# Staging buffers for the first MLP's weights, and the rank of attention's loads, in a fused attention and two-MLP kernel

## The chip, the cores and the metric

The kernel runs on one core of a Trainium2 chip. The metric is the device time of one execution in microseconds. In the profile PE is TensorE (matmuls; PEld are its weight loads), DVE is VectorE, ACT is ScalarE, POOL is GpSimd, and SP is SyncE, which here issues nearly all DMAs.

## What is computed

The reference, cut to what matters (the token axis is B * S = 2304, the model axis H * D = 512):

```python
def attn(q, k, v, M_prev, z_prev, beta):          # B, H, S, D = 4, 8, 576, 64
    scores = where(causal, -1e9, q @ k.T / sqrt(D))
    a = softmax(scores)                            # over the keys
    local = a @ v
    q_p = phi(q)                                   # x > 0 ? x + 1 : exp(x)
    mem_out = (q_p @ M_prev) / (q_p @ z_prev + 1e-6)
    g = sigmoid(beta)
    return g * mem_out + (1 - g) * local

x = attn(...).transpose(0, 2, 1, 3).reshape(2304, 512)
h = x @ w_in;   x = (h * sigmoid(h)) @ w_out              # 512 -> 2048 -> 512
h = x @ w_in2;  y = (h * tanh(softplus(h))) @ w_out2
```

## The kernel before

**An order written out beforehand.** The program adds its operations to a plan, each with a priority (the smallest goes first), the engines that could do it with a cost, and the data that it writes and reads. `Plan.issue` then plays the plan through once with these costs and fixes the order of instructions on every engine. On an engine, that which is ready earliest goes first, and of several that are ready the one with the lowest priority value. A DMA is issued on SP as soon as its data and its destination are free, by the same rule; in the plan, transfers follow each other at 360 bytes per ns. The order is fixed when the program is built; on the chip each engine takes its instructions in that order and waits where an input is late.

**Attention** goes in visits of a pair of heads: 16 visits to the first 256 queries (two steps of 128 each), then 16 to the rest (three steps). For a visit, `load_kq` loads keys and queries and `load_vm` values and memory matrix, each into one of a few buffers; the loads for visit v + 1 are asked for in the first step of visit v. A step has three stages: scores, their softmax and a DMA transposition of the result (`stage_a`), the second product three steps later (`stage_b`), the output (`stage_c`). Results go through the DRAM tensor `xd`. Attention's priorities are `att_prio(n) = 2.3 * n`, some -1.5e5 lower for the first eight steps, which are those that chunk 0 of the MLP needs.

**The MLPs** take the 2304 tokens in nine chunks of 256 each. For a chunk, `chunk_x` loads x from `xd` and splits it in a high and a low half (f16); eight times per chunk `gemm1` makes two blocks of hidden units, `hidden` their activation, and `gemm2` adds their product into the output. Their matmuls have the priorities 1e6 and up, so they fill TensorE where attention leaves it free; all the rest of an MLP has -1e6 and up, ahead of attention.

**The weights** of each MLP come as 16 units of 1 MB in a 64-bit format, eight for the first matrix (k = 0) and eight for the second (k = 1). `weight_unit` loads a unit into a staging buffer of 8 KB per partition and turns it into f32 in six passes on ScalarE and VectorE, the last of which takes the largest square sum and writes into the staging buffer; its result stands in `slot(l, u + 2)` of the MLP's weight tile. When the eight units of a half are there, `weight_scale` finds a scale for all of them, and `weight_split` writes unit u as two f16 halves into `slot(l, u)`, reading `slot(l, u + 2)`. So the weight tile `w` has 18 slots, and those of the late units lie empty at first. The units of the first MLP have priorities -2e5 + u (first half, ahead of attention) and -1e5 + u (second half, behind the first eight steps of attention and ahead of the later ones); those of the second MLP 1e5 + u, into a tile that takes attention's place.

The staging buffers are two rings: the first half of the first MLP takes the two buffers `ws` and two places in the tiles `g` and `xh`, which are not used yet; everything else takes turns in the two of `ws`. The change touches the rings (line 237), the choice of a ring in `weight_unit` (line 660) and the priorities of the two loads in `attention` (lines 787 and 792).

Of the kernel before, what the change touches and what calls it, by code (L numbers as in the profile page):

```python
# [9 lines left out]
F32 = mybir.dt.float32  # L10
F32R = mybir.dt.float32r
U32 = mybir.dt.uint32
# [26 lines left out]
NU = NF  # L39
SPARE = 2  # L40
# [138 lines left out]
def attn_moe_moe2_kernel(ctx: ExitStack, tc: tile.TileContext, kq, vm, beta, w1, w2, out):  # L179
# [22 lines left out]
    def buf(name, shape, dt, n=1):  # L202
        ts = [sb.tile([128, *shape], dt, name=f"{name}_{i}") for i in range(n)]
        return ts

    def ring(tiles):
        state = [0]

        def take():
            state[0] += 1  # L210
            return tiles[(state[0] - 1) % len(tiles)]

        return take
# [14 lines left out]
    w_first, = buf("w", [(NU + SPARE) * 2048], F16)  # L228
# [5 lines left out]

    ws = buf("ws", [1024, 2], U32, 2)
    early = [t[:, 0:4096].bitcast(U32).rearrange("p (n t) -> p n t", t=2) for t in (g_tile, xh)]
    wstages = [ring(ws + early), ring(ws)]
    ga = buf("ga", [2 * TOK], F32, 2)

    spares = [w_first[:, 2048 * NU + 1024 * i:2048 * NU + 1024 * i + 1024].bitcast(F32) for i in range(2 * SPARE)]  # L240
# [55 lines left out]
    def slot(l, u):  # L296
        return (w_first, w_second)[l][:, 2048 * u:2048 * u + 2048]
# [38 lines left out]
    def act(prio, out, in_, func, scale=1.0, bias=0.0):  # L336
        plan.add(prio, [c_act(out, in_, func, scale, bias)], [out], aps(in_, scale, bias) + [tables])

    def ts(prio, out, in0, s1, op0, s2=None, op1=None):
        plan.add(prio, [c_ts(out, in0, s1, op0, s2, op1)], [out], aps(in0, s1), shared=not ps(in0))  # L340

    def stt(prio, out, in0, s, in1, op0, op1):
        plan.add(prio, [c_stt(out, in0, s, in1, op0, op1)], [out], aps(in0, s, in1), shared=not ps(in0) and not ps(in1))

    def tt(prio, out, in0, in1, op, es=("DVE",)):
        plan.add(prio, [(*c_tt(e, out, in0, in1, op), WAIT_R * i) for i, e in enumerate(es)], [out], aps(in0, in1),
                 shared=not ps(in0) and not ps(in1))
# [34 lines left out]
    def dma(prio, out, in_, writes=None, reads=None):  # L382
        nbytes = 128 * cols(out) * SIZE[out.dtype]
        plan.add(
            prio, [("SP", 475, lambda: nc.sync.dma_start(out=out, in_=in_))],
            [out] if writes is None else writes, [in_] if reads is None else reads, tail=nbytes / 360)
# [49 lines left out]
    def load_kq(v, prio):  # L436
        p, _, nk = VISITS[v]
        n = min(S, 128 * nk)
        t = kqr()
        rk[v], rq[v] = t[:, 0, 0:n], t[:, 1]  # L440
        dma(prio, t[:, :, 0:n], kq[p].rearrange("p (t s) -> p t s", t=2)[:, :, 0:n], reads=[])

    def load_vm(v, prio):
        p, _, nk = VISITS[v]
        n = nk * 2 * (D + 1)
        t, rm[v] = rvr()[:, 0:n], rmr()
        rv[v] = t.rearrange("p (n e d) -> p n e d", n=nk, e=2)
        dma(prio, t, vm[p, :, 130:130 + n], reads=[])
        dma(prio, rm[v], vm[p, :, 0:130], reads=[])
# [43 lines left out]
    def prep_phi(v, i0, i1, prio):  # L493

        if v not in er:
            er[v] = er_()
        e, src = er[v][:, 64 * i0:64 * i1], rq[v][:, 64 * i0:64 * i1]
        act(prio, e, src, AF.Exp)
        act(prio, src, src, AF.Relu)
        stt(prio, e, e, 1.0, src, ALU.min, ALU.add)  # L500
# [65 lines left out]
    def stage_b(n, prio):  # L566

        v, qt = STEPS[n]
        R = min(128, S - 128 * qt)
        nk = qt + 1  # L570
        v1, v2, gvv = vv[v]
        vb = bank[6 + qt % 2]
        if qt < 4:
            pw = pts.pop(n).rearrange("p (s e k) q -> p s k e q", s=2, e=2)
        else:
            pw = pts.pop(n).rearrange("p (s k) (e q) -> p s k e q", s=2, e=2)
        ms = []
        for e in range(2):
            o = vb[0:R, 65 * e:65 * e + 65]
            for kb in range(nk):  # L580
                hi, lo = pw[:, 0, kb, e, :], pw[:, 1, kb, e, :]
                ms += [
                    (o, hi, v1[:, kb, e, :], kb == 0, False),
                    (o[:, 0:D], hi, v2[:, kb, e, :], False, False),
                    (o, lo, v1[:, kb, e, :], False, kb == nk - 1)]
        mm(prio, ms + [(vb[0:R, 130:260], er[v][:, 128 * qt:128 * qt + R], rm[v], True, True)])
        if not last(n):
            return
        m = 1 + qt % 2
        g = banks[0:R, 512 * 6:512 * 8].rearrange("p (b c) -> p b c", b=2)[:, 0:m, 0:260].rearrange("p b (a c) -> p b a c", a=4)  # L590
        den, t4, x = denr()[0:R, 0:m], t4r()[0:R, 0:m], xr()[0:R, 0:m]
        each = lambda y: y[0:R].unsqueeze(1).to_broadcast([R, m, 4])
        tt(prio, den, g[:, :, :, D], each(eps), ALU.add)
        other(prio, "DVE", 165, lambda: nc.vector.reciprocal(out=den, in_=den), [den], [den])
        tt(prio, den, den, each(gvv), ALU.mult)
        tt(prio, t4, g[:, :, :, 0:D], den.unsqueeze(3).to_broadcast([R, m, 4, D]), ALU.mult)
        tt(prio, x, t4[:, :, 0:2], t4[:, :, 2:4], ALU.add, ("POOL", "DVE"))
        xts[n] = (x, R)

    def stage_c(n, prio):  # L600

        if not last(n):
            return
        v, qt = STEPS[n]
        p = VISITS[v][0]
        x, R = xts.pop(n)
        m = 1 + qt % 2
        for i in range(m):
            x2, o = x[:, i].rearrange("p e d -> p (e d)"), bank[6 + i][:, 260:260 + R]
            plan.add(prio, [("PE", 56, lambda o=o, x2=x2: nc.tensor.transpose(o, x2, ident[0:R, 0:R]))], [o], [x2, ident],  # L610
                     edge=(107, 56))
        xo = xor_()[:, 0:m * R]
        copy(prio, xo.rearrange("p (b c) -> p b c", b=m),
             banks[:, 512 * 6:512 * 8].rearrange("p (b c) -> p b c", b=2)[:, 0:m, 260:260 + R])
        b, hp = divmod(p, H // 2)
        t0, n = column(b, 256 * (qt // 2)), m * R
        dma(prio, xd[128 * hp:128 * hp + 128, t0:t0 + n], xo, writes=[("xd", hp, hp + 1, t0, t0 + n)])
# [35 lines left out]
    def weight_unit(l, u, prio):  # L653

        r, w = wstages[int(l > 0 or u >= NU // 2)](), slot(l, u + SPARE).bitcast(F32)  # L660
        t = w.bitcast(U32)
        dma(prio, r, W[l][u].bitcast(U32).rearrange("p (n t) -> p n t", t=2), reads=[])
        low, high = r[:, :, 0], r[:, :, 1]
        act(prio, w, high.bitcast(F32), AF.Abs, 2.0**-112)
        ts(prio, t, t, 3, ALU.logical_shift_left)
        stt(prio, t, high, 0x80000000, t, ALU.bitwise_and, ALU.bitwise_or)
        act(prio, low, low, AF.Copy, 2.0**-29)
        tt(prio, t, t, low, ALU.add, ("DVE", "POOL"))
        top = topw[l][:, u:u + 1]

        plan.add(prio, [("ACT", 0.833 * 1024 + 200, lambda: nc.scalar.activation(  # L671
            out=low.bitcast(F32), in_=w, func=AF.Square, accum_out=top))], [top, low], [w, tables])
# [91 lines left out]
    A_RATE, MOE_B, L_V = 2.3, -1e6, 0.0  # L764
    att_prio = lambda n, d=0: A_RATE * (n + d) + (ATT_B if n < N0 else 0)
# [9 lines left out]
    def attention(n0, n1, sbs):  # L775

        for n in range(n0, n1):
            if 0 <= n - LAG - 1 < NS:
                stage_c(n - LAG - 1, att_prio(n - LAG - 1, D_C))
            if 0 <= n - LAG < NS:  # L780
                stage_b(n - LAG, att_prio(n - LAG, D_B))
            if n < NS:
                pr_ = att_prio(n)
                v, qt = STEPS[n]
                qts = VISITS[v][1]
                if qt == qts[0] and v + 1 < len(VISITS):
                    load_kq(v + 1, pr_)
                stage_a(n, sbs, pr_)
                if qt == qts[0]:
                    prep_v(v, att_prio(n, D_B) - D_V)  # L790
                    if v + 1 < len(VISITS):
                        load_vm(v + 1, att_prio(n, L_V))
                if qt == 0 and 2 in qts:
                    prep_q(v, 1, att_prio(n + 2) - D_Q)
                if qt == qts[0]:
                    prep_phi(v, 2 * qts[0], min(2 * qts[-1] + 2, S // 64), att_prio(n, D_B) - D_P)
                if qt == qts[-1] and v + 1 < len(VISITS):
                    prep(v + 1, att_prio(n + 1) - D_K)
# [20 lines left out]
    while n_att < N0:  # L819
        attention(n_att, n_att + 1, s_all)  # L820
        n_att += 1
# [96 lines left out]
```

## Time and profile before

| | us |
|---|---|
| time, median of 3 runs (1025.13 to 1026.48) | 1025.33 |
| the profiled execution: time | 1025.4 |
| the profiled execution: span from the first to the last instruction | 1023.6 |
| PE busy | 948.2 (93%) |
| PEld busy | 732.2 (72%) |
| DVE busy | 673.4 (66%) |
| ACT busy | 642.5 (63%) |
| POOL busy | 273.9 (27%) |

The mean granted clock of TensorE is 0.960 of full speed. Busy shares are means over stages that differ; where the time goes is read from the slices of the span, the table of windows and the waits.

### The profile page before, as it was taken

Reading aid. Unit: us, or ns where it says so; the run is one execution under the profiler, and the core shown is the slowest. Engines: PE = TensorE matmul, PEld = TensorE weight load, DVE = VectorE, ACT = ScalarE, POOL = GpSimd, SP = SyncE. Lnnn points to the kernel's source line nnn. Section 1 sums busy time; section 2 is a strip of 40 time slices with the busy share of each in tenths; the row PEclk is TensorE's granted clock in tenths of the full one; section 3 lists DMA queues with packets and bytes.
Section 4 is the critical chain, followed back from the end, with each engine's and each line's share of the span. In section 5 each row is a group of like instructions: output and inputs, shape, how many; then the busy total and the mean of one; then the engine's idle time right before and its main releaser. Section 6 shows DMA issues by size and latency. Waiting matters only on the chain.

```text
span 1023.6 us, 20794 instructions
## 1 busy us (share of the span) xinstructions
PE 948.2 (93%) x8364; PEld 732.2 (72%) x8364; DVE 673.4 (66%) x1231; ACT 642.5 (63%) x1095; POOL 273.9 (27%) x280
## 2 busy tenths in 40 slices
PE   2436589999999999999999999999999999999998
PEld 1225478888888888888888888766676766766665
DVE  6988687787787878777757756754544545544433
ACT  7977665666666756756667676744555545555544
POOL 1110123343343433432322522212212122222221
PEclk9956589999999999999999999999999999999999
DMA  9767924775787767845353341100100101000000
GB/s 322 230 148 208 228 58 114 162 187 133 183 156 150 151 137 148 176 114 130 105 199 104 104 146 61 42 30 14 42 22 21 32 12 42 22 21 22 1 21 21
DMA packets 149904, 107.93 MB, mean 105 GB/s; under 512 B 111152, under 2 KB 139312, under 8 KB 145712
## 3 DMA queue, kind: packets, MB, share of 16 engines
q1 hardware_dynamic: 149664, 106.60, 40.1%
q8 instruction: 65, 1.06, 0.4%
q14 instruction: 31, 0.25, 0.1%
q10 hardware_dynamic: 144, 0.00, 0.0%
HBM read 66.21 MB, written 14.16 MB: 79 GB/s over the span
## 4 chain that ended last, share of the span: by engine, by line
PE 85%; DMA 6%; DVE 4%; ACT 4%; issue 1%; SPq 0%; POOL 0%; DVEq 0%; POOLq 0%; ACTq 0%
PE banks L375 84%; DMA arena<-arena 2%; DVE w L322 1%; PE banks L610 1%; DMA g<-w 1%; ACT w L314 1%; DMA xs<-xd 1%; ACT arena L314 1%; DMA ws<-w 1%; DVE arena L322 1%; DMA arena<-kq 1%; ACT ws L671 0%; DVE w L328 0%; DVE arena L328 0%; DMA arena<-vm 0%
## 5 line engine op out<-in xcount | busy, mean ns | idle before, releaser
L375 PEld LDWEIGHTS <-w 128*128 128x128 f16 x3456 | 334.8, 98 | 43.3 <-issue 4.2
L375 PEld LDWEIGHTS <-arena 128*128 128x128 f16 (+1 forms) x3168 | 225.5, 101 | 80.1 <-DMA arena<-arena 27.5
L328 POOL TENSOR_TENSOR g<-ga,g 128x512 f16<-128x512 f32 x108 | 144.1, 1335 | 345.7 <-ACT g L314 327.4
L375 PE MATMUL banks<-xh,w 128*128 128x256 f16 x1728 | 213.8, 275 | 2.6 <-DVE ga L322 2.6
L375 PE MATMUL banks<-g,w 128*128 128x256 f16 x1728 | 209.8, 273 | 0.1
L375 PE MATMUL banks<-xh,arena 128*128 128x256 f16 x1728 | 198.6, 273 | 0.0
L375 PE MATMUL banks<-arena,g 128*128 128x512 f16 x864 | 197.4, 379 | 0.0
L375 PE MATMUL banks<-arena 128*128 128x65 f16 (+6 forms) x1728 | 119.0, 235 | 62.1 <-DMA arena<-arena 24.1
L375 PEld LDWEIGHTS <-g 128*128 128x128 f16 x864 | 84.5, 98 | 87.6
L314 ACT ACTIVATE ga<-ga 128x512 f32<-128x512 f32 x108 | 67.6, 628 | 77.5 <-DVE ga L319 53.6
L314 ACT ACTIVATE arena<-arena 128x256 f32<-128x256 f32 (+6 forms) x180 | 101.5, 592 | 18.5 <-PE banks L375 9.5
L322 DVE SCALAR_TENSOR_TENSOR ga<-ga,banks 128x512 f32<-128x512 f32 x108 | 73.7, 683 | 54.2 <-ACT ga L314 53.7
L322 DVE SCALAR_TENSOR_TENSOR arena<-arena 128x256 f16<-128x256 f32 (+6 forms) x144 | 106.1, 746 | 3.9 <-ACT arena L314 3.4
L314 ACT ACTIVATE w<-w 128x512 f32<-128x512 f32 x108 | 66.6, 625 | 47.3 <-DVE w L319 26.3
L314 ACT ACTIVATE arena<-banks,arena 128x128 f32<-128x128 f32 (+4 forms) x144 | 73.9, 545 | 33.9 <-DVE arena L546 25.9
L314 ACT ACTIVATE g<-ga 128x512 f16<-128x512 f32 x106 | 66.3, 626 | 28.7 <-DVE ga L322 28.2
L328 POOL TENSOR_TENSOR arena<-arena 128x256 f32<-128x256 f32 (+1 forms) x48 | 44.0, 916 | 139.1 <-DVE arena L328 89.3
L314 ACT ACTIVATE ga<-banks,xsc 128x512 f32<-128x512 f32 x72 | 49.2, 685 | 49.2 <-PE banks L375 45.5
L546 DVE TENSOR_REDUCE arena<-banks 128x2 f32<-128x256 f32 (+3 forms) x80 | 64.3, 804 | 23.8 <-PE banks L375 19.9
L328 POOL TENSOR_TENSOR g<-w,g 128x512 f16<-128x512 f32 x36 | 41.6, 1156 | 126.2 <-ACT g L314 126.2
L375 PEld LDWEIGHTS banks<-arena 128*128 128x128 f32 (+2 forms) x288 | 42.4, 228 | 32.9 <-ACT arena L314 29.6
L319 DVE TENSOR_SCALAR ga<-banks,xsc 128x512 f32<-128x512 f32 x36 | 27.0, 750 | 51.7 <-PE banks L375 51.6
(95 smaller groups left out, 942.0 us busy)
## 6 DMA issues: line engine op xcount, KB each, us to landing
ws<-w SPq DMA_DIRECT2D x28, 1024.0 KB, 5.3
arena<-kq SPq DMA_DIRECT2D x16, 576.0 KB, 5.0
arena<-vm SPq DMA_DIRECT2D x16, 325.0 KB, 3.4
xs<-xd SPq DMA_DIRECT2D x9, 512.0 KB, 4.6
yd<-w SPq DMA_DIRECT2D x36, 128.0 KB, 1.9
xs<-yd SPq DMA_DIRECT2D x9, 512.0 KB, 3.8
arena<-kq SPq DMA_DIRECT2D x16, 256.0 KB, 3.4
xd<-arena SPq DMA_DIRECT2D x32, 128.0 KB, 2.5
```

Of the source, the lines that this page charges most:

```text
L314: return ("ACT", ns, lambda: nc.scalar.activation(out=out, in_=in_, func=func, scale=scale, bias=bias))
L319: return ("DVE", ns, lambda: nc.vector.tensor_scalar(out=out, in0=in0, scalar1=s1, scalar2=s2, op0=op0, **kw))
L322: return ("DVE", 1.04 * cols(out) + 160, lambda: nc.vector.scalar_tensor_tensor(out=out, in0=in0, scalar=s, in1=in1, op0=op0, op1=op1))
L328: return (e, ns, lambda: eng.tensor_tensor(out=out, in0=in0, in1=in1, op=op))
L375: nc.tensor.matmul(out=o, lhsT=l, rhs=r, start=a, stop=z)
L546: other(prio, "DVE", 1.04 * cols(both) + 146, lambda: nc.vector.tensor_reduce(out=m1, in_=both, axis=AX, op=ALU.max, negate=True), [m1], [ ...
L610: plan.add(prio, [("PE", 56, lambda o=o, x2=x2: nc.tensor.transpose(o, x2, ident[0:R, 0:R]))], [o], [x2, ident], edge=(107, 56))
```

## The change

The ring of the first MLP's staging buffers becomes a written list of 16 places, one for each unit in turn. `room[0]` to `room[4]` are pairs of slots of the weight tile itself: slots 8 and 9, 10 and 11, 12 and 13, 14 and 15, 16 and 17. Units 0 to 7 go to the two of `ws`, to `g` and `xh`, and to `room[1]` to `room[4]`, so each has a place of its own. Units 8 to 15 go to `ws` (2), `room[3]`, `room[4]`, `room[0]`, `ws` (2) and `room[0]`. A place in `room` can be loaded when what stood in its slots has been read: `room[0]` after the splits of units 6 and 7 and, the second time, after unit 12. The second MLP's units take turns in the two of `ws`, as before. And the two loads of attention for the next visit get priorities that are lower by 1e6, which puts them ahead of the weights' loads wherever both are ready.

```diff
     ws = buf("ws", [1024, 2], U32, 2)
     early = [t[:, 0:4096].bitcast(U32).rearrange("p (n t) -> p n t", t=2) for t in (g_tile, xh)]
-    wstages = [ring(ws + early), ring(ws)]
+
+    room = [w_first[:, 2048 * i:2048 * i + 4096].bitcast(U32).rearrange("p (n t) -> p n t", t=2) for i in range(8, NU + SPARE, 2)]
+    wstages = [ring(ws + early + room[1:] + ws + [room[3], room[4], room[0]] + ws + [room[0]]), ring(ws)]
...
-        r, w = wstages[int(l > 0 or u >= NU // 2)](), slot(l, u + SPARE).bitcast(F32)
+        r, w = wstages[l](), slot(l, u + SPARE).bitcast(F32)
...
                 if qt == qts[0] and v + 1 < len(VISITS):
-                    load_kq(v + 1, pr_)
+                    load_kq(v + 1, pr_ - 1e6)
                 stage_a(n, sbs, pr_)
                 if qt == qts[0]:
                     prep_v(v, att_prio(n, D_B) - D_V)
                     if v + 1 < len(VISITS):
-                        load_vm(v + 1, att_prio(n, L_V))
+                        load_vm(v + 1, att_prio(n, L_V) - 1e6)
```

## Rows read from the trace of the kernel before

**Rows 1.** Page, the span in 40 slices, busy tenths of TensorE.

```profile
PE   2436589999999999999999999999999999999998
```

**Rows 2.** Windows: us, then busy time and instructions of each engine.

```profile
9.00:60.00 51.00, 19.07 (x117) 12.63 (x118) 47.86 (x86) 50.10 (x82) 2.92 (x5) 0.88 0.78 252
60.00:118.00 58.00, 33.82 (x216) 23.60 (x215) 47.85 (x102) 41.08 (x78) 7.02 (x10) 0.56 0.75 207
118.00:131.60 13.60, 6.51 (x40) 4.33 (x41) 7.61 (x30) 7.48 (x14) 1.29 (x3) 0.50 0.86 189
131.60:200.00 68.40, 68.08 (x660) 56.75 (x659) 51.85 (x117) 42.17 (x90) 19.64 (x21) 0.97 0.49 113
```

The columns of such a row are PE, PEld, DVE, ACT and POOL, then the granted clock, the DMA share and GB/s.

**Rows 3.** Waits of TensorE from 131 us on: total, times, longest.

```profile
PE banks L375 <- DVE ga L322: 2.6, 1, 2.6
```

**Rows 4.** Chain that ended last: start, length, what, four of its pieces.

```profile
3.54 10.51 DMA g<-w
...
102.48 7.48 DMA ws<-w
...
114.34 6.75 DMA arena<-arena
...
131.59 26.32 PE banks L375 x229
```

**Rows 5.** Timeline of TensorE: start, length, instruction; GEMM1 of chunk 0.

```profile
93.38 5.74 PE L375 MATMUL banks<-xh,w 128*128 128x256 f16 x42
```

**Rows 6.** Timeline of SP: weight loads and the first transposition.

```profile
2.59 0.91 SPq L385 DMA_DIRECT2D ws<-w  x2
...
4.01 0.43 SPq L385 DMA_DIRECT2D xh<-w  x1
...
14.11 3.75 SPq L559 DMA_TRANSPOSE arena<-arena  x2
...
36.04 0.33 SPq L385 DMA_DIRECT2D ws<-w  x1
...
66.01 0.35 SPq L385 DMA_DIRECT2D ws<-w  x1
...
102.48 0.34 SPq L385 DMA_DIRECT2D ws<-w  x1
```

**Rows 7.** Staging tile, 60 to 118 us: ns min/median/max, first and last start.

```profile
L671 ACT ACTIVATE ws<-w x8: 1108/1146/1167, 64.8 to 116.6; 128x1024 f32<-128x1024 f32 x8
L671 ACT ACTIVATION_READ_ACCUMULATOR ws<-w x8: 178/192/212, 65.8 to 117.6; 128x1 f32 x8
```

**Rows 8.** Waits of ScalarE, 60 to 118 us.

```profile
ACT ws L671 <- DVE w L328: 4.8, 3, 3.1
ACT w L314 <- DMA ws<-w: 4.6, 4, 2.7
```

**Rows 9.** Waits of VectorE, 60 to 118 us.

```profile
DVE w L328 <- ACT ws L314: 2.5, 2, 1.5
...
DVE w L319 <- ACT w L314: 1.2, 2, 1.1
```

**Rows 10.** Windows of attention's tile alone, columns as in rows 2.

```profile
60.00:118.00 58.00, 24.70 (x148) 16.50 (x141) 23.15 (x71) 17.80 (x47) 7.02 (x10) 0.56 0.75 207
...
131.60:200.00 68.40, 17.93 (x184) 11.82 (x178) 29.74 (x83) 22.77 (x59) 5.71 (x11) 0.97 0.49 113
```

**Rows 11.** Windows of the mask's tile alone: TensorE, then POOL.

```profile
60.00:118.00 58.00, 3.44 (x18) 0.00 (x0) 0.56 0.75 207
...
131.60:200.00 68.40, 3.14 (x22) 0.00 (x0) 0.97 0.49 113
```

**Rows 12.** Tile of x (a staging place), 0 to 20 us: its load.

```profile
DMA to landing us min/median/max: 12.5/12.5/12.5
```

**Rows 13.** Timeline of ScalarE: the first pass over a unit.

```profile
9.15 1.12 ACT L314 ACTIVATE w<-ws 128x1024 f32<-128x1024 f32 x1 [1.79 <-DMA ws<-w]
```

**Rows 14.** Tile of the scales: of the second MLP, on VectorE.

```profile
L641 DVE RECIPROCAL wsc<-cvec x2: 144/148/153, 549.4 to 629.3; 128x1 f32<-128x1 f32 x2
```

**Rows 15.** Attention's tile, 636 to 700 us: GEMM2 of the second MLP.

```profile
L375 PE MATMUL banks<-arena,g x116: 378/379/380, 653.5 to 699.9; 128*128 128x512 f16 x116
```

**Rows 16.** Timeline of TensorE: the first product with transposed data.

```profile
19.70 1.10 PE L375 MATMUL banks<-arena 128*128 128x65 f16 x8 [12.54 <-DMA arena<-arena]
```

**Rows 17.** Timeline of VectorE: the first use of that product's result.

```profile
37.81 0.16 DVE L328 TENSOR_TENSOR arena<-banks,eps 128x8 f32<-128x8 f32 x1
```

## The prediction

> **What bounds the kernel now.** I read the page's slices first, to see where TensorE is not full; then a table of windows, the waits, and the chain that ended last. TensorE is nearly idle or half busy in the first five or so slices of the span and full in almost all the rest [rows 1]. In numbers: it is busy 33.82 of 58 us between 60 and 118 us, 6.51 of 13.6 us up to 131.6 us, and 68.08 of 68.4 us after that [rows 2]. After 131 us its longest wait is 2.6 us [rows 3]. So once the first MLP runs, the remaining work of TensorE sets the end, and only two things can move it: the moment at which the MLP becomes able to fill TensorE (131.6 us now), and how much attention has been done by then.
>
> What sets that moment is the preparation of the first MLP's weights. The chain of waits runs through the load of a late unit (7.48 us at 102.48), then through a transposition for the last attention step that delays the scale of the second half (6.75 us at 114.34), to the unbroken run of matmuls at 131.59 [rows 4]. The first hidden activations were ready to be computed long before: GEMM1 of chunk 0 starts at 93.38 [rows 5]. GEMM2 lacks the second half of the weights.
>
> **What the loads cost now.** The first four loads are issued from 2.59 us on; the second half has two buffers, so after the load at 36.04 the next can be issued only at 66.01, and the last of the half at 102.48 (six loads in 36.5 us) [rows 6]. All eight units of that half have their square sums between 65.8 and 117.6 us [rows 7]. In 60 to 118 us ScalarE waits 4.6 us for such loads and 4.8 us for VectorE's step of the same unit, and VectorE 2.5 and 1.2 us for ScalarE's steps of the same unit [rows 8, 9]: with one unit at hand at a time, the two engines wait for each other. VectorE, the fuller one, is busy 47.85 of 58 us there, so 10.15 us are idle [rows 2].
>
> **The change, part by part.**
>
> *Five buffers in the second half.* Units 8 and 9 go to the two old buffers, 10 and 11 to places that hold staged units 6 and 7 before, so all four can be in place before 60 us. Unit 12 needs the splits of units 6 and 7, units 13 and 14 need 8 and 9 done, unit 15 needs unit 12. From 60 us on there are two or more units to choose from until the last. The gain is bounded below by nothing, if attention's own chain is what VectorE really follows, and above by the whole idle time, 10.15 us. The two waits on ScalarE for the same unit make 3.7 us of it; the rest are waits in attention, which a second unit at hand can fill. I take the middle, 7 us, and leave 3 us for unit 15, whose load and steps come one after the other.
>
> *Attention moved behind the weights.* The second half is ranked ahead of attention from step 8 on. Now it can use that rank, so some steps move past the start of the MLP. In 60 to 118 us VectorE spends 23.15 us on attention [rows 10] for nine steps (18 mask matmuls, two to a step) [rows 11]: 2.6 us each. In 131.6 to 200 us TensorE spends 17.93 us [rows 10] on eleven steps (22 mask matmuls) [rows 11]: 1.63 us each, at the full clock. Every step moved frees 2.6 us before the start and costs 1.63 us after it: 0.95 us gained. If no step moves, the term is 0; if eight do (8 to 15, which no one needs until chunk 1), 7.6 us. I take four: 3.9 us.
>
> *Eight buffers in the first half.* All eight loads are issued at once. Two neighbours at the start land 2.46 us apart (3.54 + 10.51 = 14.05 us for the third [rows 4]; 4.01 + 12.5 = 16.5 us for the fourth [rows 6, 12]). ScalarE has three passes over a unit, the last of them 1.15 us long [rows 7], and is 50.10 of 51 us busy between 9 and 60 us [rows 2]; the loads do not hold it up, so earlier ones give nothing there: 0. If its cover, the full ScalarE, were gone, a gain of at most the 0.9 us of idle time in that window would be had.
>
> *Attention's loads first.* At the start the load of visit 1's keys and queries, its values and its memory matrix, and one memory matrix more go ahead of the first weight: four more issues of some 0.47 us (two weights take 0.91 us in [rows 6]), 1.9 us. The first weight's pass starts at 9.15 us after a wait of 1.79 us for the load [rows 13], so it becomes some 1.8 us later. Visit 1's own passes are then there to fill ScalarE, so the cost lies between 0 and 1.8 us; I take 1.8. Later in the kernel the rank only decides which of several ready loads goes first on SP; after 131 us TensorE never idles over 2.6 us at once [rows 3], so I put nothing there, at most that wait.
>
> The sum is made against the profiled execution, 1025.4 us (span 1023.6), within 0.1 us of the median of 1025.33: 1025.4 - 7.0 - 3.9 + 1.8 = 1016.3 us.
>
> **What is late next.** The second MLP's weights. The scale of their second half is ready at 629.3 us [rows 14], its first GEMM2 starts at 653.5 us [rows 15]. The scale, then a split, leaves about 20 us. A start of the MLP 9 us earlier uses half of this.
>
> **A row and a rule that speak against it.** The first transposition is issued at 14.11 us, when four loads of 1 MB are under way [rows 6], and TensorE waits 12.54 us for it, until 19.70 [rows 16]; the fourth load landed at 16.5. So a transposition waits for what is queued in front of it. With eight loads in front, at 2.46 us each, the queue ends about four loads or 9.8 us later, and the first transpositions and visit 2's load land near 30 us. VectorE needs the first result of attention's second product only at 37.81 us now [rows 17], so 8 us of cover remain, and the sum puts nothing on it.
>
> The Trainium skill, page "DMA: Bandwidth & Descriptors", section "Queues, rings and completion order", says that each DMA engine consumes a queue's descriptors in ring order. By that rule, ranking attention's loads first helps only those that are ready before the weights are issued; the trace agrees as far as the 12.54 us go. The sum by it would be that of the rival of the queue, below.
>
> **Rivals.**
>
> *The queue (slower).* The order on each engine is written out beforehand. If an attention instruction that depends on a late transposition stands ahead of weight passes on VectorE or ScalarE, these wait behind it. It decides from a stall of 9.1 + 2.05 = 11.2 us on. That would need the 9.8 us of additional queue to hit an engine with no cover, and once more for visit 2 or 3, say 13 us together: 1025.4 - 9.1 + 13 = 1029 us. For it: 12.54 us of such a wait exist already. Against: it falls on TensorE, which has nothing else to do, and the 8 us of cover. 0.14.
>
> *Attention bounds the start (same).* Steps 0 to 7 slide by the queue's 9.8 us, and with them x of chunk 0 (GEMM1 at 93.38 becomes 103) and everything ranked below; the units fill holes but the start stays within 2 us of 131.6, at 1025 us. Against: attention is ranked ahead of the second half and finds free engines earlier, as the first half's units end sooner. 0.12.
>
> *Second MLP late (smaller gain).* Attention ends later by more than the 20 less 9 us of slack; each microsecond above is lost. With 5 lost, 1021 us. Against: attention keeps its rank, and VectorE has a quarter of its time free in 131.6 to 200 us (51.85 of 68.4 us busy, [rows 2]). 0.12.
>
> *All of it (larger gain).* All 10.15 us close, eight steps move, and the early loads cost nothing: 1025.4 - 10.15 - 7.6 = 1007.6 us. 0.17.
>
> The forecast's own case has 0.45, between 1011 and 1020 us.
>
> **How the numbers follow.** The likeliest is 1016.3 us. The range has to hold 8 in 10: with 0.10 left out at the top (most of the queue's case) and little below, it runs from 1007 to 1027 us. A measurement of this kernel tells 0.2% from no change, here 2.05 us. Faster than 1023.3 us: the forecast's 0.45, the larger gain's 0.17, the late second MLP's 0.12, 0.74 in all. Slower than 1027.4: 0.14. Same: 0.12.
>
> **What the profile after would show.** Right: loads of the second half issued before 60 us, the last of the eight done near 100 us rather than 118, the unbroken run of matmuls from about 115 us, full TensorE from there to the end, and fewer mask matmuls before that start. ScalarE's waits for loads and for VectorE's step of the same unit near nothing. Wrong: the run starting after 125 us; idle VectorE or ScalarE behind a transposition between 15 and 45 us; a wait of TensorE for a split of the second MLP near 640 us; or the start moved by as much as forecast with as many microseconds of deferred attention on TensorE behind it.

## The result, and the profile after

The changed kernel takes 1016.73 us (median of 4 runs, 1014.98 to 1017.62), beside 1025.88 us for the kernel before: ratio 0.9909, 95% interval 0.9891 to 0.9927. The forecast was 1016.3 us. The profiled execution took 1014.98 us, span 1013.1 us, 10.5 us less than the span of before. Line numbers after the added lines are 2 higher, so helper L375 is now L377.

The windows of the kernel after (columns as in [rows 2]):

```profile
9.00:60.00 51.00, 13.93 (x89) 9.51 (x89) 45.85 (x81) 47.80 (x74) 3.32 (x5) 0.92 0.92 285
60.00:97.00 37.00, 12.24 (x81) 8.33 (x82) 35.18 (x62) 29.85 (x49) 4.53 (x5) 0.50 0.74 230
60.00:118.00 58.00, 32.16 (x260) 24.16 (x261) 52.16 (x101) 46.66 (x79) 10.78 (x10) 0.66 0.61 180
112.60:200.00 87.40, 84.27 (x817) 69.71 (x816) 59.81 (x153) 55.48 (x128) 23.02 (x29) 0.96 0.53 118
```

From 60 us until the last unit is done (97 us), VectorE is busy 35.18 of 37 us; before it left 10.15 of 58 us idle up to 118 us [rows 2]. But TensorE, full from the MLP's start on before, now has 3.13 us of holes between 112.6 and 200 us, and a mean granted clock of 0.96 there.

Where the units went: the square sums of the second half (staging places in `ws`, then those in the weight tile), first and last start in 60 to 100 us, on ScalarE:

```profile
L673 ACT ACTIVATION_READ_ACCUMULATOR ws<-w x4: 180/186/216, 69.2 to 91.9; 128x1 f32 x4
...
L673 ACT ACTIVATION_READ_ACCUMULATOR w<-w x4: 176/182/190, 76.3 to 96.5; 128x1 f32 x4
```

The last one starts at 96.5 us, 21 us earlier than the 117.6 of [rows 7]. The waits of ScalarE that answer to [rows 8], in 60 to 109 us:

```profile
ACT w L316 <- DMA w<-w: 2.2, 1, 2.2
...
ACT w L673 <- DVE w L330: 1.4, 2, 0.8
```

Once for a load (2.2 us, unit 15) instead of 4.6 us, and 1.4 us instead of 4.8 for VectorE's step of the same unit. The waits of VectorE for ScalarE's steps of the same unit, 2.5 and 1.2 us in [rows 9], are one of 0.2 us in the same window:

```profile
DVE w L321 <- ACT w L316: 0.2, 1, 0.2
```

GEMM2 of chunk 0, the first matmul from `g`, in 90 to 145 us, in the kernel before and after:

```profile
L375 PE MATMUL banks<-g,w x54: 272/273/273, 138.5 to 144.9; 128*128 128x256 f16 x54
```

```profile
L377 PE MATMUL banks<-g,w x131: 269/273/273, 112.6 to 144.9; 128*128 128x256 f16 x131
```

It starts 25.9 us earlier, and the span shrinks by 10.5. The other 15.4 us are found with two more views. First, the mask's matmuls up to GEMM2's start, two to a step of attention (columns as in [rows 11]), before and after:

```profile
0.00:138.50 138.50, 7.68 (x40) 0.97 (x4) 0.70 0.73 214
```

```profile
0.00:112.60 112.60, 5.21 (x28) 0.97 (x4) 0.79 0.78 238
```

14 steps have been begun instead of 20. Six steps at the prediction's 1.63 us are, by estimate, 9.8 us of TensorE's time that now lie behind the start. Second, the windows of 152 to 168 us, after:

```profile
152.00:156.00 4.00, 3.27 (x34) 2.57 (x32) 1.43 (x4) 2.32 (x5) 0.17 (x1) 1.00 1.55 210
156.00:160.00 4.00, 1.96 (x8) 1.17 (x8) 3.43 (x7) 1.86 (x6) 0.37 (x1) 0.74 0.57 136
160.00:164.00 4.00, 3.78 (x28) 2.78 (x29) 2.53 (x14) 3.52 (x7) 0.79 (x1) 0.50 0.25 66
164.00:168.00 4.00, 4.00 (x35) 3.43 (x34) 2.96 (x7) 2.21 (x7) 0.93 (x2) 0.91 0.57 135
```

and TensorE's timeline there:

```profile
156.26 0.95 PE L377 MATMUL banks<-arena 64*128 64x256 f32 x4 [0.99 <-ACT arena L316]
157.14 0.28 PE L377 MATMUL banks<-mask,ident 128*128 128x128 bf16 x2
159.04 0.79 PE L377 MATMUL banks<-diag,onesf 128*128 128x128 f32 x2 [1.61 <-DVE diag L330]
```

The matmul with `diag` belongs to the scale of chunk 1's x (`largest`). That x had its load issued only at 151.06 us, since the steps it needs came late. 3.0 us are idle in these four windows: 1.61 us before the matmul with `diag`, and 0.99 us before a step of attention that waits for ScalarE. (That chunk 1's matmuls would have filled the second hole, had x been there, is argued and not shown by itself.) The granted clock falls to 0.50 (the 1.2 GHz level) between 160 and 164 us. By estimate, at the clock of these windows the busy time loses 1.96 x 0.26 + 3.78 x 0.50 + 4.00 x 0.09 = 2.8 us. So 25.9 - 9.8 - 3.0 - 2.8 = 10.3 us, against 10.5 us of the spans. That is closer than the parts are known: the four executions of this kernel lie 2.6 us apart.

### The profile page after: what moved, and what is told of

Same layout as the page of the kernel before. It is cut to its first block, busy times and chain, and to the rows that moved or that the text cites. A ratio compares the mean times of both kernels' runs of the same rounds, so it can differ in the third digit from the quotient of the medians.

```text
span 1013.1 us, 20798 instructions
## 1 busy us (share of the span) xinstructions
PE 936.3 (92%) x8364; PEld 725.9 (72%) x8364; DVE 669.0 (66%) x1231; ACT 643.8 (64%) x1097; POOL 263.9 (26%) x278
## 3 DMA queue, kind: packets, MB, share of 16 engines
q8 instruction: 65, 1.06, 0.4%
## 4 chain that ended last, share of the span: by engine, by line
PE 86%; ACT 5%; DMA 4%; DVE 3%; issue 1%; SPq 0%; POOL 0%; ACTq 0%; DVEq 0%; POOLq 0%
PE banks L377 85%; ACT w L316 2%; DMA ws<-w 2%; PE banks L612 1%; DVE w L324 1%; ACT arena L316 1%; ACT ws L673 1%; DMA xs<-xd 1%; ACT w L673 1%; DMA arena<-arena 1%; ACT ws L316 1%; DMA arena<-kq 0%; DMA w<-w 0%; DVE arena L330 0%; DVE arena L324 0%
## 5 line engine op out<-in xcount | busy, mean ns | idle before, releaser
L377 PEld LDWEIGHTS <-w 128*128 128x128 f16 x3456 | 333.4, 98 | 40.9 <-issue 2.9
L377 PEld LDWEIGHTS <-arena 128*128 128x128 f16 (+1 forms) x3168 | 224.5, 101 | 60.9 <-DMA arena<-arena 17.2
L330 POOL TENSOR_TENSOR g<-ga,g 128x512 f16<-128x512 f32 x108 | 141.3, 1309 | 331.9 <-ACT g L316 314.7
L377 PE MATMUL banks<-g,w 128*128 128x256 f16 x1728 | 210.9, 273 | 1.0 <-POOL g L330 0.9
L377 PE MATMUL banks<-xh,w 128*128 128x256 f16 x1728 | 209.9, 273 | 0.6 <-DVE ga L324 0.6
L377 PE MATMUL banks<-xh,arena 128*128 128x256 f16 x1728 | 199.1, 273 | 0.0
L377 PE MATMUL banks<-arena,g 128*128 128x512 f16 x864 | 197.6, 379 | 0.0
L377 PE MATMUL banks<-arena 128*128 128x65 f16 (+7 forms) x1728 | 112.2, 230 | 53.1 <-ACT arena L316 32.0
L377 PEld LDWEIGHTS <-g 128*128 128x128 f16 x864 | 84.5, 98 | 87.4
L316 ACT ACTIVATE w<-w 128x512 f32<-128x512 f32 (+2 forms) x124 | 84.2, 691 | 56.9 <-DVE w L321 31.0
L324 DVE SCALAR_TENSOR_TENSOR arena<-arena 128x640 f16<-128x640 f32 (+6 forms) x144 | 108.6, 762 | 9.5 <-ACT arena L316 9.1
L316 ACT ACTIVATE arena<-arena 128x512 f16<-128x512 f32 (+6 forms) x181 | 102.7, 590 | 18.3 <-PE banks L377 10.1
L377 PEld LDWEIGHTS banks<-arena 64*128 64x128 f32 (+2 forms) x288 | 38.7, 215 | 43.2 <-ACT arena L316 40.0
```

Source lines behind the costliest of these rows:

```text
L316: return ("ACT", ns, lambda: nc.scalar.activation(out=out, in_=in_, func=func, scale=scale, bias=bias))
L324: return ("DVE", 1.04 * cols(out) + 160, lambda: nc.vector.scalar_tensor_tensor(out=out, in0=in0, scalar=s, in1=in1, op0=op0, op1=op1))
L330: return (e, ns, lambda: eng.tensor_tensor(out=out, in0=in0, in1=in1, op=op))
L377: nc.tensor.matmul(out=o, lhsT=l, rhs=r, start=a, stop=z)
```

## The experiments

Each experiment was timed in five rounds beside the kernel before; ratios are to it. "GEMM2" is the start of GEMM2 of chunk 0 in the profile, "steps" the steps of attention begun by then. "Rest" is what the span has above an account from the kernel before: GEMM2's start, plus the 885.1 us that follow it there (1023.6 - 138.5), plus 1.63 us for each step short of 20. GEMM2, steps, span and rest come from one profiled execution of each kernel; the executions of one kernel lie 1 to 7 us apart, so a rest of 2 or 3 us tells little.

| kernel | median us | ratio (95%) | GEMM2 us | steps | span us | rest us |
|---|---|---|---|---|---|---|
| before | 1025.88 | 1 | 138.5 | 20 | 1023.6 | 0 |
| after | 1016.73 | 0.9909 (0.9891 to 0.9927) | 112.6 | 14 | 1013.1 | 5.6 |
| e1_no_rank | 1018.01 | 0.9933 (0.9915 to 0.9952) | 117.1 | 13 | 1014.1 | 0.5 |
| e2_rank_only | 1023.38 | 0.9971 (0.9961 to 0.9981) | 130.7 | 19 | 1020.7 | 3.3 |
| e3_second_two | 1024.08 | 0.9981 (0.9970 to 0.9992) | 137.0 | 21 | 1021.7 | 1.2 |
| e4_first_four | 1019.23 | 0.9929 (0.9914 to 0.9944) | 120.6 | 16 | 1015.5 | 3.3 |
| e5_steps12 | 1018.60 | 0.9930 (0.9915 to 0.9945) | 126.6 | 18 | 1016.9 | 1.9 |
| e6_rank_visit1 | 1020.97 | 0.9961 (0.9946 to 0.9976) | 131.0 | 18 | 1018.9 | -0.5 |
| e7_rank_later | 1027.95 | 1.0020 (1.0006 to 1.0033) | 139.1 | 19 | 1027.3 | 1.5 |
| e8_plan_925 | 1024.27 | 0.9985 (0.9973 to 0.9997) | 138.9 | 20 | 1022.2 | -1.8 |
| e10_after_925 | 1015.60 | 0.9907 (0.9889 to 0.9925) | 113.4 | 14 | 1013.4 | 5.1 |
| e11_after_visit1 | 1018.53 | 0.9930 (0.9912 to 0.9947) | 111.4 | 14 | 1014.9 | 8.6 |
| e12_seven | 1014.15 | 0.9893 (0.9873 to 0.9913) | 108.4 | 12 | 1011.0 | 4.5 |
| e13_seven_visit1 | 1010.59 | 0.9856 (0.9836 to 0.9876) | 108.1 | 13 | 1009.1 | 4.5 |

**One part undone: the rank.**

```diff
-                    load_kq(v + 1, pr_ - 1e6)
+                    load_kq(v + 1, pr_)
...
-                        load_vm(v + 1, att_prio(n, L_V) - 1e6)
+                        load_vm(v + 1, att_prio(n, L_V))
```

> The changed kernel with attention's loads at their old rank; the buffers stay. Theory (the second half's five buffers carry the gain; the rank only delays the first weight): the first weight pass of ScalarE starts near 9.2 us instead of 12.28, and the time is that of the changed kernel or up to 3 us less, 1013 to 1017 us. Rival (the rank is needed, because eight early loads would otherwise stand in front of visit 1's loads): attention's second visit starts after 28 us, and the time is 1019 us or more.

The first weight's pass starts at 9.39 us, as the theory has it, but the time is not lower: 0.9933 beside 0.9909. The two intervals overlap. GEMM2 starts 4.5 us later than with the rank. So a cost of the rank does not show, and a gain is not shown either. The theory's upper end (1017 us) is passed by 1 us. The rival's first sign came, for visit 1's scores start at 32.87 us on TensorE (7.29 us with the rank), but its 1019 us is not reached.

**One part alone: the rank** (the same two lines, in the kernel before).

> The kernel before with attention's loads ranked first, nothing else. Theory: the four issues ahead of the first weight cost 0 to 3 us, 1025 to 1029 us; the second half's loads are spread as before. Rival (the rank carries the gain): 1017 to 1021 us.

Theory and rival were both wrong: it is faster by 0.29% (the interval lies below 1), and GEMM2 starts 7.8 us earlier, with the buffers of before. The first weight's pass starts at 11.76 us, so the delay that I charged is there, and something else more than pays for it.

**The second half in two buffers.**

```diff
-    wstages = [ring(ws + early + room[1:] + ws + [room[3], room[4], room[0]] + ws + [room[0]]), ring(ws)]
+    wstages = [ring(ws + early + room[1:] + 4 * ws), ring(ws)]
```

> The changed kernel, but the second half of the weights takes turns in two buffers as before (eight in the first half and the rank stay). Theory: nearly all of the gain is gone, 1023 to 1028 us, and GEMM2 of chunk 0 starts near 138 us. Rival (the eight early loads carry the gain): 1016 to 1019 us, and GEMM2 starts near 113 us.

As the theory has it: 1024.08 us, and GEMM2 at 137.0 us. Of the changed kernel's 0.91%, 0.72 points go with the five buffers, and the two intervals lie far apart. What is left, 0.19%, is no more than the rank brings alone. Between 60 and 118 us VectorE's waits for ScalarE's steps of the same unit are back, 3.8 us as before (3.7 us in [rows 9]):

```profile
DVE w L330 <- ACT ws L316: 2.0, 2, 1.8
DVE w L321 <- ACT w L316: 1.8, 4, 1.0
```

ScalarE's waits for loads (2.0 us) and for VectorE's step of the same unit (0.9 us) stay small here, and the gain is gone all the same. VectorE idles 9.65 of these 58 us again. So the idle time that counts is VectorE's, not ScalarE's.

**The first half in four places.**

```diff
-    wstages = [ring(ws + early + room[1:] + ws + [room[3], room[4], room[0]] + ws + [room[0]]), ring(ws)]
+    wstages = [ring(ws + early + ws + early + ws + [room[3], room[4], room[0]] + ws + [room[0]]), ring(ws)]
```

> The changed kernel, but the first half takes turns in four places as before (five in the second half and the rank stay). Theory: the gain stays, 1014 to 1019 us, and GEMM2 of chunk 0 starts between 110 and 118 us; with a shorter queue SP's issues at 9 to 30 us take no longer than 2 us each. Rival (the eight early loads carry the gain): 1023 to 1028 us.

Most of the gain stays (0.9929; the median, 1019.23 us, is 0.23 us above the theory's range). GEMM2 starts at 120.6 us, later than expected; 16 steps have been begun by then instead of 14. One point was wrong: SP still needs 5.65 us for the transposition at 9.54 us. The places of units 10 and 11 are empty from the start here, so both are loaded at once and six loads stand in front, not four. But the number of loads does not explain it: at 30.50 us, with four loads issued shortly before (26.91 to 28.66 us), an issue takes 5.79 us.

```profile
6.83 1.93 SPq L387 DMA_DIRECT2D w<-w  x2
8.89 0.55 SPq L387 DMA_DIRECT2D arena<-kq  x1
9.54 5.65 SPq L561 DMA_TRANSPOSE arena<-arena  x1
...
30.50 5.79 SPq L561 DMA_TRANSPOSE arena<-arena  x1
```

**Twelve steps of attention ranked ahead of the second half.**

```diff
-    att_prio = lambda n, d=0: A_RATE * (n + d) + (ATT_B if n < N0 else 0)
+    att_prio = lambda n, d=0: A_RATE * (n + d) + (ATT_B if n < 12 else 0)
```

> The changed kernel, with the first twelve steps of attention ranked ahead of the second half's weights (eight in the changed kernel). Theory (GEMM2's start and the steps done by then trade at 2.6 us of VectorE before against 1.63 us of TensorE after, and the late x of chunk 1 costs the changed kernel some 6 us near 155 to 164 us): GEMM2 starts 4 to 10 us later than 112.6 us, more steps are done by then, the wait and the half clock near 155 us are gone, and the time is 1012 to 1018 us. Rival (the earliest possible start of GEMM2 is what counts): the time rises by the whole delay, 1021 to 1027 us.

GEMM2 starts 14.0 us later than in the changed kernel, with four more steps done, and the time is only 1.9 us longer (the two intervals overlap). Four steps are, by estimate, 6.5 us; the wait near 155 us is gone:

```profile
155.00:160.00 5.00, 4.45 (x46) 3.56 (x47) 4.24 (x13) 3.72 (x9) 1.51 (x2) 1.00 0.38 74
160.00:165.00 5.00, 5.00 (x55) 4.08 (x52) 3.84 (x11) 2.67 (x7) 1.58 (x2) 1.00 0.24 68
```

Here TensorE idles 0.55 us and keeps the full clock, which gives back 5.3 of the changed kernel's 5.8 us. 14.0 - 6.5 - 5.3 = 2.2 us, against 1.9 us between the medians and 3.8 us between the two profiled spans. So the exchange (a step done late costs its 1.63 us on TensorE, and the hole near 155 us goes with the late x of chunk 1) fits, and the rival's 1021 us and more do not come. The start and the time lie a little beyond what the theory gave (4 to 10 us, at most 1018 us).

**The rank for visit 1 alone, and for all others alone** (in the kernel before).

```diff
-                    load_kq(v + 1, pr_)
+                    load_kq(v + 1, pr_ - 1e6 * (v == 0))
...
-                        load_vm(v + 1, att_prio(n, L_V))
+                        load_vm(v + 1, att_prio(n, L_V) - 1e6 * (v == 0))
```

> The kernel before, with only visit 1's loads ranked first. Theory (the gain of the rank alone comes from the first ten microseconds, where visit 1's passes fill the wait for the first weight): the time of the kernel with the whole rank, 1021 to 1024.5 us. Rival (it comes from later loads): 1025 to 1028 us.

> The kernel before, with the rank for the loads of all visits but visit 1. Theory (the rank acts at the start only): 1025 to 1027 us, first weight pass at 9 to 10 us. Rival (later loads carry it): 1021 to 1024 us.

The second kernel has `(v > 0)` in both lines. Visit 1 alone is faster by 0.39% (1020.97 us, at the lower end of the theory's range) and moves GEMM2 to 131.0 us; all other visits alone leave it at 139.1 us and make the kernel 0.20% slower (1027.95 us, 0.95 us above the theory's range; the first pass starts at 9.93 us, as expected). Both rivals did not come. So in the kernel before the rank acts in the first microseconds. The window of 0 to 9 us, in the kernel before, then with visit 1 ranked first:

```profile
0.00:9.00 9.00, 2.62 (x13) 1.38 (x13) 3.21 (x13) 3.65 (x8) 3.03 (x23) 1.00 0.69 224
```

```profile
0.00:9.00 9.00, 4.29 (x21) 2.69 (x22) 3.60 (x17) 5.32 (x14) 3.06 (x23) 1.00 0.73 229
```

ScalarE does 5.32 us of work instead of 3.65 while the first weight is still on its way. The weight's own pass moves from 9.15 [rows 13] to 10.80 us, 1.65 us, for 1.67 us of work done ahead. This makes the rank free, not a gain; how the 4 us come about behind this start I did not settle.

**An edit without a meaning**, in the kernel before and in the changed one.

```diff
-    LAT = {"PE": 197, "ACT": 150, "DVE": 135, "POOL": 90, "SP": 920}
+    LAT = {"PE": 197, "ACT": 150, "DVE": 135, "POOL": 90, "SP": 925}
```

> The kernel before, with 925 ns in place of 920 for a DMA's latency in the plan: nothing about the work or its ranks changes, only near ties in the written order. Theory (a gain of 2 to 3 us, as of the rank alone or of the early eight loads, is no larger than what a rewritten order brings by itself): the time moves by 1 to 3 us to one side or the other. Rival (such an edit moves nothing, so 2 to 3 us mean something): 1025 to 1027 us.

> The changed kernel, with 925 ns in place of 920 for a DMA's latency in the plan. Theory (a rewritten order alone moves this kernel by some 2 us): 1014 to 1020 us. Rival (it moves nothing): within 1 us of the changed kernel.

The kernel before moves by 0.15%, as its theory has it; the changed one by nothing that can be told (0.9907 beside 0.9909), as its rival has it. A rewritten order alone can be worth 1.5 us, and one edit in two kernels does not show how much more it can be. The five buffers' 7.4 us stand clear of that. Visit 1's 4 us in the kernel before are above it, but not by much. The eight early loads (0.9929 to 0.9909, 2.1 us faster; from e2 to e3, 1.0 us slower) and the rank within the changed kernel (0.9933 to 0.9909, 2.5 us) are not told from it.

**The changed kernel with the rank for visit 1 alone** (the two lines of e6).

> The changed kernel, with only visit 1's loads ranked first. Theory (the rank helps at the start and does nothing or harm later): 1013 to 1017 us. Rival (with the buffers, the later loads need the rank): 1018 us or more.

GEMM2 starts earliest yet of the kernels with these buffers, 111.4 us, but the time is 1018.53 us, the rival's side. Its interval overlaps that of the changed kernel. The rest, 8.6 us, is the largest of all; from GEMM2's start to 1000 us TensorE idles 9.2 us (5.3 in the changed kernel, 1.6 in the kernel before), 4.5 of them for `diag` of a chunk's x:

```profile
PE banks L377 <- DVE diag L330: 4.5, 3, 2.3
```

**Seven places for the second half**, with the whole rank and with visit 1's.

```diff
-    wstages = [ring(ws + early + room[1:] + ws + [room[3], room[4], room[0]] + ws + [room[0]]), ring(ws)]
+    wstages = [ring(ws + early + room[1:] + ws + [room[3], room[4]] + early + [room[0], ws[0]]), ring(ws)]
```

> The changed kernel, with units 12 and 13 of the second half in the places in g and xh, 14 in room 0 and 15 in a buffer of ws, so that unit 15 no longer waits for unit 12 and its load (issued at 85.02 us in the changed kernel) comes some 10 us earlier. Theory (what is left of VectorE's idle time is the lone last unit, some 3 us): GEMM2 of chunk 0 starts up to 6 us earlier than 112.6 us, and as steps move behind it the time is 1013 to 1017 us. Rival (the loads no longer hold anything up): GEMM2 starts as in the changed kernel, 1016 to 1019 us.

> The places of the run with seven buffers in the second half, and only visit 1's loads ranked first. Theory (both small gains add): 1011 to 1015 us. Rival (x of chunk 1 comes too late for a still earlier start): 1016 to 1019 us, with TensorE waiting near 150 to 165 us.

The last load of the half is issued at 68.81 us instead of 85.02, the last square sum starts at 93.0 us instead of 96.5, and GEMM2 at 108.4 us: 1014.15 us, in the theory's range, but its interval overlaps that of the changed kernel. With visit 1's rank it is 1010.59 us, a little below the theory's 1011 us, ratio 0.9856 to the kernel before; its interval (0.9836 to 0.9876) lies below the changed kernel's (0.9891 to 0.9927). So this version is faster than the kernel before and than the changed one. Between 150 and 165 us TensorE still idles 2.3 us there (3.0 in the changed kernel), but its waits from 100 us on have no `diag` among the largest:

```profile
PE banks L377 <- DVE xh L324: 1.1, 1, 1.1
PE banks L377 <- DVE ga L324: 0.6, 1, 0.6
```

That the two small gains add is not what happened: visit 1's rank alone lost 0.2 points with five buffers (e11) and wins 0.4 with seven, in both cases with intervals that overlap. Which order of the engines makes this difference, if it is one, stays open.

## Why the prediction was right, point by point

*What sets the end.* Right in kind. GEMM2's start and the steps done by then account for all kernels within -1.8 to 8.6 us, and the largest rests stand where TensorE idles most behind the start (e11). But 8.6 us is nearly as much as the whole gain, so these two things alone do not give the time. TensorE was also not "full from there to the end", as the prediction wanted it. And the start moved further than forecast. Its mark was the long run of matmuls at 131.59 us [rows 4], forecast near 115; the chain after has it here, 22.3 us earlier:

```profile
109.34 16.38 PE banks L377 x153
```

*Five buffers and the steps moved behind the weights (7.0 and 3.9 us).* Together 10.9 us forecast; undoing the buffers (e3) takes 0.72 points, 7.4 us. The mechanism is the one described: VectorE's two waits for ScalarE's steps of the same unit, 3.7 us, became 0.2 us (3.8 us again in e3), and VectorE's idle time fell to 1.8 us by the last unit, less than the 3 us that I left. What was too large is the second term. Against e3, GEMM2 starts 24.4 us earlier with seven steps fewer. By the prediction's prices, an estimate, seven steps are 18.2 us of this, so 6.2 us are left for the first term, beside 7.0 forecast. The second term is 7 x 0.95 = 6.7 us, from which the late x takes 5.8: 0.9 us are left, beside 3.9 forecast. "No one needs them until chunk 1" was true of their place and wrong in time: chunk 1's x came late, with 3.0 us of idle time and 2.8 us of lowered clock, and these were not in the sum. That too many steps moved is not shown: e5 puts four back and is not faster, and e12 and e13, with 12 and 13 steps, have the two lowest medians.

*Eight buffers in the first half (0).* 2.1 us between e4 and the changed kernel, within overlapping intervals and near what a rewritten order gives. Not told from nothing.

*Attention's loads first (a cost of 1.8 us).* The term that failed, in its sign. The delay was read rightly and even too small in the changed kernel, where the first pass moves by 3.1 us:

```profile
12.28 1.12 ACT L316 ACTIVATE w<-ws 128x1024 f32<-128x1024 f32 x1 [2.28 <-DMA ws<-w]
```

But I took the upper bound of a cost whose lower bound I had put at nothing, "visit 1's own passes are then there to fill ScalarE". They fill it, and in the kernel before the rank alone gives 3.0 us (e2), with visit 1 only 4.0 us (e6); how, stays open, and in the changed kernel its 2.5 us are not told from nothing. So the sum came out near the measurement by luck: errors offset each other. Taken one after the other along the runs, the rank gives 3.0 us (e2; forecast: a cost of 1.8), the eight buffers then cost 1.0 (e3; forecast: 0), and the five buffers with the moved steps give 7.4 (the changed kernel; forecast: 10.9). That is 9.4 us in all, where 9.1 were forecast.

*The queue.* The first transpositions are late as forecast. TensorE's first product of transposed data and VectorE's first use of it, after:

```profile
32.00 1.13 PE L377 MATMUL banks<-arena 128*128 128x65 f16 x8
```

```profile
40.28 0.16 DVE L330 TENSOR_TENSOR arena<-banks,eps 128x8 f32<-128x8 f32 x1
```

32.00 us where 19.70 was [rows 16] and near 30 was expected; 40.28 where 37.81 was [rows 17]. The transposition issued at 14.79 us landed 16.2 us later, at 31.0, just behind the last of the eight weight loads (30.4 us). The rule of the Trainium skill, page "DMA: Bandwidth & Descriptors", section "Queues, rings and completion order", that each DMA engine consumes a queue's descriptors in ring order, agrees with this.

But the queue is only a part of the reason, and the prediction read the 12.54 us of [rows 16] wrongly. The transposition for which TensorE waited until 19.70 us was issued only at 14.11, so no more than 5.6 us of that wait passed in the queue. Before that, SP itself waited. In the traces SP's 330 DMAs tell their landing by eight semaphores in turn, and none is issued before the one eight places ahead of it has landed. So loads of 1 MB at the head hold back the issues behind them, which the plan does not know. SP's waits for such landings, in the kernel before (up to 131 us) and after (up to 60 us); L559 and L561 issue the transpositions:

```profile
SPq L385 <- DMA ws<-w: 3.5, 2, 1.8
...
SPq L559 <- DMA g<-w: 2.1, 1, 2.1
```

```profile
SPq L387 <- DMA ws<-w: 2.3, 1, 2.3
...
SPq L561 <- DMA ws<-w: 2.1, 1, 2.1
```

Without the rank (e1) eight issues in a row, from 9.39 to 26.79 us, each leave within 0.1 us of such a landing; the first transposition is among them, at 24.29 us, and TensorE stands 22.7 us for it before visit 1's scores. All this cost little: between 9 and 60 us VectorE and ScalarE are busy 2.0 and 2.3 us less than before, of which ScalarE's wait for the first weight alone is 2.28 us.

*The second MLP.* Its second half's scale is ready at 628.3 us, GEMM2 starts at 645.9: 17.6 us of the 24.2 between [rows 14] and [rows 15] are left, and TensorE waits little there (1.06 us idle in 600 to 640 us, none in 640 to 660). Right, and not the bound.

*The rivals.* The queue (slower) and attention as the bound of the start (same) did not come. The larger gain did not come with this edit; e13, at 1010.59 us, comes within 3 us of its 1007.6.

## What to carry to other kernels

When two engines pass one piece of work to and fro, look at what each waits for: if each waits for the other's step of the same piece, a buffer for a second piece can give the idle time back, and an array whose final content is not there yet can be that buffer. Then ask what moves behind the work that now comes first: each step deferred must still be paid on the engine that bounds the rest, and the first consumer of the deferred steps may be nearer than it looks. Count, too, how many transfers the issuing engine lets be under way at once (eight here): large loads at the head take these places from small ones behind them. And time an edit without a meaning once, so that gains of 1 or 2 us from a rewritten order are not taken for causes.

## What was not expected of the hardware

SP's issue of a DMA is not always short. In the changed kernel the eight loads of 1 MB land between 12.26 and 30.44 us, and two issues in that time take 4.37 and 7.85 us of SP's time:

```profile
9.39 3.21 SPq L387 DMA_DIRECT2D w<-w  x2
14.79 1.31 SPq L561 DMA_TRANSPOSE arena<-arena  x1
17.29 4.37 SPq L387 DMA_DIRECT2D arena<-vm  x1
21.75 0.57 SPq L387 DMA_DIRECT2D arena<-kq  x1
22.41 7.85 SPq L561 DMA_TRANSPOSE arena<-arena  x1
30.36 0.54 SPq L387 DMA_DIRECT2D arena<-vm  x1
30.99 1.21 SPq L561 DMA_TRANSPOSE arena<-arena  x1
32.30 1.01 SPq L387 DMA_DIRECT2D ws<-w  x2
```

Once the loads are through, a transposition takes 1.21 us again. Everything behind on SP is held up with it; the next two weight loads leave from 32.30 us on. What makes an issue long is not shown. The transposition at 14.79 us, with six loads under way, takes 1.31 us, and in e1 the issue at 9.39 us, with seven under way, takes 0.57 us.

The granted clock also did not follow TensorE's holes in a way that I can tell. In the changed kernel it falls to 0.50 after 3 us of idle time near 156 us; with seven places and the whole rank (e12), TensorE is less busy over 150 to 165 us, and the clock stays full in the profiled execution:

```profile
150.00:165.00 15.00, 10.33 (x98) 7.40 (x94) 10.09 (x32) 9.66 (x24) 3.54 (x5) 1.00 0.71 151
```

```profile
150.00:165.00 15.00, 12.02 (x93) 8.63 (x91) 10.08 (x28) 9.53 (x22) 2.13 (x3) 0.77 0.74 132
```

The first row is e12, the second the changed kernel. The order of the program need not be the reason. Over whole executions of e12 alone the mean granted clock lies between 0.971 and 0.999; in the changed kernel's four it is 0.971 to 0.973.
